# Another engine for some tiles of the first batch, and an uneven split of the last output tile

## The chip, the cores and the metric

One core of a Trainium2 chip. The metric is device time in microseconds (us), lower is better. The kernel before takes 251.05 us (median of three runs, 250.95 to 251.22).

## The reference, cut to what matters

```python
a = softmax(phi)                                   # 8 batches, 8 heads, 576 rows, 32 memory slots
k_m, v_m = a^T k, a^T v                            # per head 32 x 64
x = softmax(q k_m^T / 8) v_m                       # -> [8, 576, 512]
out = x + relu(layernorm(x) @ w_ch1) @ w_ch2       # 512 -> 2048 -> 512
```

The kernel never forms layernorm(x) @ w_ch1 directly: it folds v_m and w_ch1 into one small matrix per batch (w1b) and multiplies that by the attention weights (Eh). The result, the 2048-wide hidden layer, is made in 16 tiles of 128 hidden units by 576 rows.

## The kernel before

The hidden tiles, and who empties them:

```python
def mm1(b, j0, j1):
    for j in range(j0, j1):
        h_ps = big([P, 2, 512], FP32, "h_ps")      # PSUM, 3 buffers in all for this tag
        ... 4 matmuls of 128 x 288 from w1b and Eh ...                        # L405
        if j % 3 or j == 0:
            nc.scalar.activation(out=dst, in_=h_ps[:, :, 0:HS], func=AF.Relu) # L411, ScalarE
        else:
            nc.vector.tensor_scalar(out=dst, in0=h_ps[:, :, 0:HS], ... max 0) # L413, VectorE
```

The first batch has no work before it to hide behind. It alternates parts of the folding with hidden tiles; the folding products use the same three buffers, and VectorE empties them (L388):

```python
mm1(0, 0, 2)
w1_mean(2); m_copy(2); a_w1b(0, 1)    # mean of w1 by TensorE, copied by ScalarE; folding: TensorE, then VectorE
mm1(0, 2, 5)
w1_mean(3); m_copy(3); a_w1b(0, 2)
mm1(0, 5, 8)
w1_mean(4); m_copy(4); a_w1b(0, 3)
a_vb(0)                               # L281, two short VectorE passes, wanted by x_tiles
mm1(0, 8, 16)
x_tiles(0, [0, 1]); x_tiles(0, [2, 3])
mm2(0, 0, 0, 4) ...                   # L474, "the long product": 40 matmuls, output tiles 0, 1 and half of 2
a_kv(1); a_tr(1); a_qT(1, 0) ...      # batch 1's k and v, then its q in two halves, as their loads land
```

The loads go in one order through GpSimd's queue: q, k, v of batch 0, w1 in five pieces, w2 in four, then phi, k, v and the two halves of q of batch 1, then batch 2. A finished output tile is stored from SyncE's queue (mm2_out). The last tile is made in two halves of 256 columns (mm2_last), so that the first half is stored while the second is computed.

The softmax here doesn't subtract the row's maximum and nothing guards it: scores larger than these inputs give would overflow.

## Time and profile before

| | before |
|---|---|
| time, median of 3 | 251.05 us |
| span of the profiled execution | 248.5 us |
| the profiled execution's own time | 250.3 us |
| TensorE busy | 96% |
| share of TensorE in the chain that ended last | 88% |

The chain is the work that ended last, followed back to what released each step. The lines themselves stand in the prediction.

### The profile page before, as it was taken

Reading aid. Unit: us, or ns where it says so; the run is one execution under the profiler, and the core shown is the slowest. Engines: PE = TensorE matmul, PEld = TensorE weight load, DVE = VectorE, ACT = ScalarE, POOL = GpSimd, SP = SyncE. Lnnn points to the kernel's source line nnn. Section 1 sums busy time; section 2 is a strip of 40 time slices with the busy share of each in tenths; the row PEclk is TensorE's granted clock in tenths of the full one; section 3 lists DMA queues with packets and bytes.
Section 4 is the critical chain, followed back from the end, with each engine's and each line's share of the span. In section 5 each row is a group of like instructions: output and inputs, shape, how many; then the busy total and the mean of one; then the engine's idle time right before and its main releaser. Section 6 shows DMA issues by size and latency. Waiting matters only on the chain.

```text
span 248.5 us, 5893 instructions
## 1 busy us (share of the span) xinstructions
PE 238.5 (96%) x2491; PEld 132.5 (53%) x2491; DVE 156.2 (63%) x304; ACT 130.0 (52%) x219; POOL 60.6 (24%) x100
## 2 busy tenths in 40 slices
PE   7879999999999999999999999999999999999993
PEld 2444555557544665467544774467444764476453
DVE  3246663785578646686569547785679538783641
ACT  3165572587463555736472646655680755465210
POOL 8643241032515402090206202170205011000000
PEclk9999999999999999999999999999999999999999
DMA  7999999998599899829975995539983302103133
GB/s 151 195 202 207 206 257 208 291 222 148 119 200 210 122 218 242 160 38 201 251 127 112 158 245 136 122 38 223 209 158 77 80 7 46 42 17 70 42 84 84
DMA packets 42450, 36.82 MB, mean 148 GB/s; under 512 B 17460, under 2 KB 37688, under 8 KB 42424
## 3 DMA queue, kind: packets, MB, share of 16 engines
q0 software_dynamic: 17776, 19.53, 46.9%
q1 hardware_dynamic: 24488, 16.79, 29.3%
q8 instruction: 19, 0.31, 0.5%
q10 hardware_dynamic: 160, 0.13, 0.2%
q14 instruction: 7, 0.06, 0.1%
HBM read 41.42 MB, written 9.44 MB: 205 GB/s over the span
## 4 chain that ended last, share of the span: by engine, by line
PE 88%; DMA 4%; DVE 2%; ACT 2%; POOL 1%; issue 1%; DVEq 0%; POOLq 0%
PE ch_ps L474 50%; PE h_ps L405 25%; DMA kv_bf<-in_v_dram 4%; PE w1b_ps L384 3%; PE kv_ps L210 2%; PE o_ps L435 2%; PE last_ps L486 1%; PE sc_ps L322 1%; PE m_ps L165 1%; ACT rT L411 1%; PE den_ps L353 1%; DVE w1b L388 1%; POOL q_bf L92 1%; ACT E_sb L327 1%; POOL kv_bf L84 1%
## 5 line engine op out<-in xcount | busy, mean ns | idle before, releaser
L474 PE MATMUL ch_ps<-w2b,rT 128*128 128x512 bf16 x560 | 128.4, 380 | 0.0
L474 PEld LDWEIGHTS <-rT 128*128 128x128 bf16 x560 | 52.0, 98 | 63.5 <-issue 6.5
L405 PE MATMUL h_ps<-Eh,w1b 128*128 128x288 bf16 x512 | 66.6, 286 | 1.3 <-ACT rT L411 1.2
L411 ACT ACTIVATE rT<-h_ps 128x576 bf16<-128x576 f32 x88 | 52.4, 648 | 28.7 <-PE h_ps L405 28.7
L405 PEld LDWEIGHTS <-w1b 128*128 128x128 bf16 x512 | 49.5, 97 | 18.3 <-issue 2.6
L388 DVE SCALAR_TENSOR_TENSOR w1b<-m_sb,rsum,w1b_ps 128x512 bf16<-128x512 f32 (+1 forms) x66 | 44.2, 726 | 9.6 <-PE w1b_ps L384 5.3
L413 DVE TENSOR_SCALAR rT<-h_ps 128x576 bf16<-128x576 f32 x40 | 30.3, 757 | 24.9 <-PE h_ps L405 24.3
L498 DVE SCALAR_TENSOR_TENSOR x_sb<-ch_ps,rstd,x_sb 128x512 f32<-128x512 f32 x35 | 26.1, 746 | 9.9 <-PE ch_ps L474 9.1
L454 DVE BATCH_NORM_STATS2 bst<-x_sb 128x6 f32<-128x512 f32 x36 | 24.4, 678 | 7.6 <-ACT x_sb L441 7.6
L441 ACT ACTIVATE x_sb<-o_ps 128x1024 f32<-128x1024 f32 (+1 forms) x20 | 17.5, 938 | 18.4 <-PE o_ps L435 18.4
L281 POOL TENSOR_TENSOR vb<-v,vmask 128x256 bf16<-128x256 bf16 x12 | 7.7, 663 | 60.1 <-DVE rs L237 60.1
L194 POOL TENSOR_TENSOR es<-e_sb 128x512 f32<-128x512 bf16 x6 | 6.9, 1156 | 62.9 <-ACT e_sb L187 62.9
L460 ACT ACTIVATE rstd<-mv,eps_sb 128x2 f32<-128x2 f32 (+1 forms) x20 | 5.9, 297 | 30.4 <-DVE mv L455 30.2
L327 ACT ACTIVATE E_sb<-sc_ps,rs 128x640 bf16<-128x640 f32 x16 | 11.8, 790 | 12.4 <-PE sc_ps L322 12.4
L369 DVE SCALAR_TENSOR_TENSOR Eh<-E_sb,rs,rden 128x576 bf16<-128x576 bf16 x16 | 12.4, 815 | 8.8 <-ACT rden L368 8.8
L384 PE MATMUL w1b_ps<-w1r,kvT 64*32 64x512 bf16 (+1 forms) x264 | 10.9, 374 | 0.0
L179 PE MATMUL w_ps<-fill 128*128 128x512 f32 (+1 forms) x16 | 9.4, 699 | 1.6 <-DVE fill L119 1.6
L227 DVE CAST k<-kv_ps 128x256 bf16<-128x256 f32 x7 | 3.0, 425 | 12.5 <-PE kv_ps L210 12.5
L187 ACT ACTIVATE e_sb<-phi_st 128x1152 bf16<-128x1152 f32 x8 | 9.2, 1151 | 2.6 <-DMA phi_st<-in_phi_dram 2.6
L368 ACT ACTIVATE rden<-rden 128x576 f32<-128x576 f32 x16 | 10.0, 672 | 0.1
L92 POOL DMA_DIRECT2D q_bf<-in_q_dram x10 | 7.6, 756 | 4.6 <-DMA w2b<-in_moe_w_ch_dram 1.8
L210 PE MATMUL kv_ps<-kv_bf,e_sb 64*32 64x128 bf16 (+1 forms) x648 | 7.4, 215 | 0.6 <-DMA kv_bf<-in_v_dram 0.3
(76 smaller groups left out, 151.3 us busy)
## 6 DMA issues: line engine op xcount, KB each, us to landing
out_dram<-x_sb SPq DMA_DIRECT2D x70, 128.0 KB, 2.8
kv_bf<-in_k_dram POOLq DMA_DIRECT2D x7, 576.0 KB, 6.1
kv_bf<-in_v_dram POOLq DMA_DIRECT2D x7, 576.0 KB, 9.2
phi_st<-in_phi_dram SPq DMA_DIRECT2D x6, 576.0 KB, 6.1
q_bf<-in_q_dram POOLq DMA_DIRECT2D x6, 576.0 KB, 13.9
w2b<-in_moe_w_ch_dram POOLq DMA_DIRECT2D x4, 512.0 KB, 17.7
w1r<-in_moe_w_ch_dram POOLq DMA_DIRECT2D x3, 512.0 KB, 13.8
q_bf<-in_q_dram POOLq DMA_DIRECT2D x4, 288.0 KB, 12.4
```

The source lines that it names most:

```text
L210: nc.tensor.matmul(ps[32 * j:32 * (j + 1), g, 0:D * (sl.stop - sl.start)], e[r:r + TS, c, j, :], kv[r:r + TS, j, sl, D * c:D * (c + 1)], s ...
L327: nc.scalar.activation(out=E_[:, g].rearrange("p (a x) -> p a x", a=2), in_=sc[:, :, 0:HP], func=AF.Exp, scale=s["rs"][:, g:g + 1])
L369: nc.vector.scalar_tensor_tensor(out=Eh[:, g, :], in0=s["E"][:, g, 0:S], scalar=s["rs"][:, g:g + 1], in1=rd[:, g].rearrange("p a x -> p (a ...
L384: nc.tensor.matmul(ps[32 * j:32 * (j + 1), g, 0:N], s["kvT"][r:r + 64, 2, 32 * j:32 * (j + 1)], w1r[r:r + 64, j, fs], start=True, stop=Tru ...
L388: nc.vector.scalar_tensor_tensor(out=s["w1b"][:, g, fs], in0=m_sb[:, fs], scalar=s["rsum"][:, g:g + 1], in1=ps[:, g, 0:N], op0=ALU.mult, o ...
L405: nc.tensor.matmul(h_ps[:, half, 0:HS], s["w1b"][:, g, P * j:P * (j + 1)], s["Eh"][:, g, HS * half:HS * (half + 1)], start=(g == 0), stop= ...
L411: nc.scalar.activation(out=dst, in_=h_ps[:, :, 0:HS], func=AF.Relu)
L413: nc.vector.tensor_scalar(out=dst, in0=h_ps[:, :, 0:HS], scalar1=0.0, scalar2=None, op0=ALU.max)
L441: nc.scalar.activation(out=x[:, 0:n].rearrange("p i (u y) -> p i u y", u=2), in_=o_ps.rearrange("p u (i y) -> p i u y", i=2)[:, 0:n], func ...
L454: nc.vector.bn_stats(out=stt, in_=x)
L474: nc.tensor.matmul(ch_ps, rT[:, j, P * t:P * (t + 1)], w2b[:, j, :], start=(j == 0), stop=(j == JC - 1))
L498: nc.vector.scalar_tensor_tensor(out=x, in0=ch_ps, scalar=rstd, in1=x, op0=ALU.mult, op1=ALU.add)
```

## The change

Its intent: VectorE folds twice between groups of hidden tiles, and the tiles that it also empties come right behind its folding, so that they wait. It is to take tiles 1, 4, 7, 10, 13 instead of 3, 6, 9, 12, 15 (batch 0 alone), and the two short passes for vb move behind tile 10. At the end, a part of 384 columns and then one of 128 leave less to do after the last matmul.

```diff
-            if j % 3 or j == 0:
+            if j % 3 != 1 if b == 0 else j % 3 or j == 0:
                 nc.scalar.activation(out=dst, ...)
...
-        for n in range(2):
+        for cs in (slice(0, 384), slice(384, 512)):
             ps = big([P, 2, 512], FP32, "last_ps")
-            cs = slice(256 * n, 256 * (n + 1))
+            N = cs.stop - cs.start
...  (256 becomes N in the matmul and in VectorE's pass)
     a_w1b(0, 3)
+    mm1(0, 8, 11)
     a_vb(0)
-    mm1(0, 8, 16)
+    mm1(0, 11, 16)
```

More of the change, by code (lines that the diff above doesn't have):

```diff
@@ L481, in mm2_last @@
         x, rstd = xs[(pr, t)]
-        for n in range(2):
+        for cs in (slice(0, 384), slice(384, 512)):
             ps = big([P, 2, 512], FP32, "last_ps")
-            cs = slice(256 * n, 256 * (n + 1))
+            N = cs.stop - cs.start
             for j in range(JC):
-                nc.tensor.matmul(ps[:, 0, 0:256], pair[pr][:, j, P * t:P * (t + 1)], w2b[:, j, cs],
+                nc.tensor.matmul(ps[:, 0, 0:N], pair[pr][:, j, P * t:P * (t + 1)], w2b[:, j, cs],
                                  start=(j == 0), stop=(j == JC - 1))
-            nc.vector.scalar_tensor_tensor(out=x[:, cs], in0=ps[:, 0, 0:256], scalar=rstd,
+            nc.vector.scalar_tensor_tensor(out=x[:, cs], in0=ps[:, 0, 0:N], scalar=rstd,
                                            in1=x[:, cs], op0=ALU.mult, op1=ALU.add)
```

## The prediction

> **What bounds the kernel now.** I read the page first: the share of busy time, then the chain of work that ended last.
>
> ```profile
> PE 238.5 (96%) x2491; PEld 132.5 (53%) x2491; DVE 156.2 (63%) x304; ACT 130.0 (52%) x219; POOL 60.6 (24%) x100
> ...
> PE 88%; DMA 4%; DVE 2%; ACT 2%; POOL 1%; issue 1%; DVEq 0%; POOLq 0%
> ```
>
> TensorE carries 88% of the chain; the second line says so, the first only that it is busy. So a change gains only where TensorE waits, or before its first and after its last matmul. Page, chain and waits put the waits in the first batch and the end. The list of waits for TensorE has one that this change is about:
>
> ```profile
> PE h_ps L405 <- ACT rT L411: 1.2, 5, 0.2
> ```
>
> Then the timeline of the first batch (start, length, engine, line, operation, count, idle before), from tile 8 of its 16 hidden tiles on:
>
> ```profile
> 28.98 1.41 DVE L388 SCALAR_TENSOR_TENSOR w1b<-m_sb,rsum,w1b_ps 128x512 bf16<-128x512 f32 x2 [1.11 <-ACT m_sb L174]
> 29.29 0.65 ACT L411 ACTIVATE rT<-h_ps 128x576 bf16<-128x576 f32 x1 [0.34 <-PE h_ps L405]
> 29.99 1.14 PE L405 MATMUL h_ps<-Eh,w1b 128*128 128x288 bf16 x8 [0.25 <-ACT rT L411]
> ...
> 30.31 0.49 DVE L281 TENSOR_TENSOR vb<-v,vmask 128x256 bf16<-128x256 bf16 x2
> 30.68 1.19 ACT L411 ACTIVATE rT<-h_ps 128x576 bf16<-128x576 f32 x2 [0.74 <-PE h_ps L405]
> 30.71 0.75 DVE L413 TENSOR_SCALAR rT<-h_ps 128x576 bf16<-128x576 f32 x1
> ...
> 31.38 2.15 PE L405 MATMUL h_ps<-Eh,w1b 128*128 128x288 bf16 x16 [0.25 <-ACT rT L411]
> ```
>
> A tile is four matmuls into one of three PSUM buffers; ScalarE or VectorE empties it, and only then may a later tile use that buffer. The instruction record gives 0.121 us from one matmul's start to the next, so 0.485 us a tile, and the first reader's start 0.69 us after the tile's. A reader keeps the buffer 0.65 us (ScalarE) or 0.75 us (VectorE); TensorE goes on 0.05 us later. "0.25 idle" is counted from modelled ends; in starts, the matmul at 31.38 follows the one at 30.84, where 30.96 was possible: 0.42 us lost. The same stands at 23.39 (0.41, and 0.21 more for its second half at 23.85, which waits for the folded weights), 26.80 (0.41) and 29.99 (0.41): 1.86 us in four places.
>
> The end, from the timeline of the last 10 us:
>
> ```profile
> 241.05 3.66 PE L486 MATMUL last_ps<-w2b,rT 128*128 128x256 bf16 x32
> 244.74 0.48 DVE L488 SCALAR_TENSOR_TENSOR x_sb<-last_ps,rstd,x_sb 128x256 f32<-128x256 f32 x1 [1.21 <-PE last_ps L486]
> ```
>
> After the last matmul, VectorE's 0.48 us and one store (issued at 245.25, landed at 247.2 on one queue and 247.45 on the other) are bare time.
>
> [...]0.25 us idle in each of four places, each ended by the reader of a buffer. [...]its ten 128-column transposes at 44.85, each with a weight load, stand 55.5 ns apart. [...]the last two stores, 64 KB each, took 1.95 and 2.19 us.
>
> **Part 1: who empties the first batch's tiles.** VectorE had tiles 3, 6, 9, 12, 15 and gets 1, 4, 7, 10, 13; five each, so nothing is added or removed. I went through the built order of both programs, which shows which reader each tile waits for, and put the durations above to it.
>
> Tiles 0 to 3 run as before: tile 1's reader ends at 21.65 in place of 21.60, and nobody waits for it. Tile 4 waits for tile 2's reader, tile 7 for tile 5's, tile 10 for tile 8's. Tiles 2, 5 and 8 are ScalarE's before and after, and start when they did (22.69, 26.10, 29.29): ScalarE's copies of the mean, at 21.76, 25.17 and 28.35, still wait for the matmuls in front of them. So three of the four stalls stay: 0.41 + 0.21 + 0.41 + 0.41 = 1.44 us.
>
> The fourth goes. Before, tile 9 (VectorE) waits behind the fold and behind vb, from 29.74 to 30.71, so tile 12 takes the buffer of tile 10 and waits for its reader to 31.33. Changed, ScalarE reads tile 9 at 29.84 to 30.49, VectorE reads tile 10 at 30.68 to 31.43, and tile 12 waits for tile 9, long done: it starts at 30.96, 0.42 us earlier. Behind it: tile 13 waits for tile 10 (31.48, where 31.45 was possible); tile 14 at 31.97 waits for tile 11's reader (31.17 to 31.82); tile 15 at 32.46 for tile 12's (31.72 to 32.37): free. vb moves behind tile 10 and ends near 31.83, before tile 13 is ready at 32.13. The products after it take tile 13's buffer (VectorE 32.17 to 32.92) and then tile 14's (ScalarE to 33.31): the second half starts near 33.36 in place of 33.80. So the next matrix product starts at about 33.69, not 34.13: 0.44 us earlier.
>
> **Part 2: what of it survives.** The same TensorE work follows, until batch 1's products with k and v at 43.07. They'd start at 42.63, but v's load lands at 42.74, on a queue that is full throughout (the page's DMA row is at 9 there) and waits for nothing that this change moves. So TensorE waits to about 42.79 and 0.28 us is left. The first half of batch 1's q lands at 44.53, its use moves from 44.85 to 44.57: just in time (its second half, landed 46.33, is wanted at 46.53). The stores that share the engines start 0.44 us earlier and may hold these loads up a little, so I count 0.25. Later loads have over a microsecond, and the chain from 53.5 to 241 is TensorE with the same waits, so this is carried to the end.
>
> **Part 3: the last tile in 384 and 128 columns.** TensorE before: 32 x 0.1095 = 3.50 us. After: 16 x 0.1625 (between 256 and 512 columns) + 16 x 0.0555 = 3.49: even. The last matmul's own length falls from 0.273 to 0.220 us (the transposes'), but it starts 0.05 later. VectorE's last pass: 484 - 128 x 1.04 = 351 ns, 0.13 us less. The store: four packets of 1 KB on each DMA engine and queue, 75 ns each; at 512 bytes half of that saves some 0.15 of about 2 us; as two queues share the engines I count 0.08. The 384 part's issue ends near 245.0, before the second's at 245.11. Together 0.21 us.
>
> **Sum.** 0.25 + 0.21 = 0.46 us; 251.05 - 0.46 = 250.6 us, 0.2%.
>
> **Rivals.** (a) *All stalls go, as the change intends*: 1.86 + 0.21, some 249.0 us. For it: the four stalls are all put down to ScalarE. Against it: the three readers that end three of them don't change. Even then the loads for batch 1 would hold TensorE at 42.74, so it could not last. (b) *The loads take it all*: if the earlier stores push v and q back by 0.2 us or more, part 1 gives 0 to 0.1 and the time is 250.8 to 251.0. For it: queues full from 20 to 54 us. Against it: the stores issued at 39.5 move no data until 43.0 by the DMA records, after v. (c) *vb or VectorE becomes the wait*: if VectorE is 0.4 us late with tile 13, the products behind it wait and part 1 is gone: 250.85. Against it: 0.3 us of slack by the working above. [...](e) *No DMA limit*: all of 0.44 stays, 250.4.
>
> **Range and chances.** (b), (d) and (e) span 250.4 to 251.0; three runs of before spread by 0.27 us. I take 250.15 to 251.05. Two per cent is 5 us, over twice what even (a) gives, and no part can cost that: within 2% at 0.98, the rest shared.
>
> **What would show it.** In the changed profile: idle before the first batch's tiles still three times, at 23.4, 26.8 and 30.0, with ScalarE named, and none near 31.4; the long product starts at 33.7; a wait of TensorE for v of batch 1 near 42.7, new in the list of waits; from there everything about 0.25 us earlier; last_ps x32 as long as before; VectorE's last pass near 0.35 us; the last store a little under 2 us. I'm wrong if the stalls at 26.8 or 30.0 are gone, if v lands earlier too, or if the 128-column matmuls stand over 60 ns apart.

What the prediction took from outside this case is cut out of it, and with it rival (d), that a 128-column matmul would take longer in the last tile than in the transposes. No term of the sum is cut: it came to 0.25 + 0.21 = 0.46 us, and the range stands without (d) too, since (b) as it was written reaches 251.0. What part 3 reckons with is in the trace of before: starts of matmuls 0.109 us apart at 256 columns (L486) and 0.216 at 512 (L474); VectorE's pass from PSUM 750 ns at 512 columns (L498) and 484 at 256 (L488), so 1.04 ns a column, and 218 ns if that line is drawn on to none; a store's packets of 2 KB 154 ns on SyncE's queue, those of 1 KB 75 there and 68 on ScalarE's (medians). The 0.03 us taken off for the stores in part 2, and the 0.15 and 0.08 us for the smaller store in part 3, are estimates.

## The result, and the profile after

| | before | changed |
|---|---|---|
| median | 251.0 us (4 runs, 250.94 to 251.22) | 250.12 us (4 runs, 249.78 to 250.62) |
| profiled execution | 250.3 us, span 248.5 | 249.78 us, span 248.0 |

The ratio is 0.9965 (95% interval 0.9947 to 0.9983). Ratios in this text are the mean time of one kernel's fast runs over that of the other's of the same rounds, so not quite the ratio of the medians. 250.12 lies 0.03 us under the predicted range. The medians are 0.88 us apart, the two profiled executions 0.52.

The shares of busy time and of the chain, after:

```profile
PE 239.1 (96%) x2491; PEld 132.3 (53%) x2491; DVE 156.5 (63%) x304; ACT 129.7 (52%) x219; POOL 60.6 (24%) x100
...
PE 79%; DMA 17%; DVE 1%; issue 1%; POOL 1%; ACT 1%; POOLq 0%
```

Busy time is as before, the chain is not: DMA has gone from 4% to 17%. The steps of the chain from 10 us to TensorE's first, in order of time (start, length, what), show where that is:

```profile
10.13 14.78 DMA w1r<-in_moe_w_ch_dram
24.91 0.29 issue
25.20 19.28 DMA q_bf<-in_q_dram
44.48 0.05 issue
44.52 0.73 PE qT_ps L304 x10
```

Before, the chain ran over TensorE with short steps of the other engines from 13 us on. Now it runs over the loads up to batch 1's q, which lands at 44.48, and TensorE takes it up 0.04 us later. The list of TensorE's waits (total, times, longest) has that wait as a new line, and the stall of the first batch went from 1.2 to 1.0 us:

```profile
PE h_ps L405 <- ACT rT L411: 1.0, 4, 0.2
...
PE qT_ps L304 <- DMA q_bf<-in_q_dram: 0.2, 1, 0.2
```

The timeline of the first batch from tile 8 on, as in the prediction:

```profile
29.07 1.19 ACT L411 ACTIVATE rT<-h_ps 128x576 bf16<-128x576 f32 x2 [0.34 <-PE h_ps L405]
29.77 3.13 PE L405 MATMUL h_ps<-Eh,w1b 128*128 128x288 bf16 x24 [0.25 <-ACT rT L411]
30.46 0.76 DVE L413 TENSOR_SCALAR rT<-h_ps 128x576 bf16<-128x576 f32 x1 [0.29 <-PE h_ps L405]
...
31.14 0.48 DVE L281 TENSOR_TENSOR vb<-v,vmask 128x256 bf16<-128x256 bf16 x2
...
33.48 8.81 PE L474 MATMUL ch_ps<-w2b,rT 128*128 128x512 bf16 x40
```

The stall before tile 10 (0.25 idle, at 29.77 now) is still there, and behind it 24 matmuls run without a break where there were 8, a stall, and 16. And the end:

```profile
240.65 3.66 PE L486 MATMUL last_ps<-w2b,rT 128*128 128x384 bf16 x32
...
244.35 0.35 DVE L488 SCALAR_TENSOR_TENSOR x_sb<-last_ps,rstd,x_sb 128x128 f32<-128x128 f32 x1 [0.22 <-PE last_ps L486]
```

TensorE's 32 matmuls take 3.66 us in both kernels, VectorE's last pass 0.35 in place of 0.48.

For comparing runs I cut each trace at six places, all read from the instruction records and the record of DMA completions. Below, "head" is the first batch's part of the change (readers and vb), "end" that of the last tile, K to Q the stretch in which batch 1's q is wanted. The places: v0, the landing of the second half of batch 0's v; M, the third matmul of tile 0; L, the start of the long product; K, batch 1's first product with k and v; Q, the first transpose of the second half of batch 1's q; E, the first matmul of the last tile.

| us | v0 lands | M | M to L | L to K | K to Q | Q to E | E to end |
|---|---|---|---|---|---|---|---|
| before | 14.51 | 19.96 | 14.17 | 8.94 | 3.73 | 194.24 | 7.45 |
| changed | 14.03 | 19.74 | 13.74 | 8.94 | 3.98 | 194.25 | 7.33 |

The head gains 0.43 (M to L), gives back 0.25 at q (K to Q), and the end gains 0.12; the other 0.22 us is M itself. Batch 0's loads had landed earlier by 0.48 us, and 0.22 of that was left at M. No instruction before M differs between the two kernels. So part of even these 0.52 us is not the change's. One of the prediction's own signs of being wrong also came up, "v lands earlier too": it landed at 42.31, not 42.74, but counted from v0 it came 28.28 us later, before 28.23. The wait for v that was to be new isn't in this trace; the one for q is.

### The profile page after: what moved, and what is told of

It is laid out like the page before. It is cut to its first block, busy times and chain, and to the rows that moved or that the text cites. A ratio compares the mean times of both kernels' runs of the same rounds, so it can differ in the third digit from the quotient of the medians.

```text
span 248.0 us, 5893 instructions
## 1 busy us (share of the span) xinstructions
PE 239.1 (96%) x2491; PEld 132.3 (53%) x2491; DVE 156.5 (63%) x304; ACT 129.7 (52%) x219; POOL 60.6 (24%) x100
## 4 chain that ended last, share of the span: by engine, by line
PE 79%; DMA 17%; DVE 1%; issue 1%; POOL 1%; ACT 1%; POOLq 0%
PE ch_ps L474 46%; PE h_ps L405 22%; DMA q_bf<-in_q_dram 8%; DMA w1r<-in_moe_w_ch_dram 6%; DMA kv_bf<-in_k_dram 3%; PE w1b_ps L384 3%; PE kv_ps L210 2%; PE last_ps L486 1%; PE o_ps L435 1%; PE sc_ps L322 1%; PE den_ps L353 1%; POOL q_bf L92 1%; DVE k L227 1%; PE qT_ps L304 0%; ACT qT L307 0%
## 5 line engine op out<-in xcount | busy, mean ns | idle before, releaser
L474 PE MATMUL ch_ps<-w2b,rT 128*128 128x512 bf16 x560 | 128.4, 380 | 0.0
L474 PEld LDWEIGHTS <-rT 128*128 128x128 bf16 x560 | 52.1, 98 | 63.4 <-issue 6.4
L498 DVE SCALAR_TENSOR_TENSOR x_sb<-ch_ps,rstd,x_sb 128x512 f32<-128x512 f32 x35 | 26.1, 746 | 9.6 <-PE ch_ps L474 8.8
L179 PE MATMUL w_ps<-fill 128*128 128x512 f32 (+1 forms) x16 | 10.3, 759 | 1.6 <-DVE fill L119 1.6
L358 ACT ACTIVATE rden<-den_ps 64x576 f32<-64x576 f32 x12 | 7.7, 644 | 0.2
```

Of the source, the lines that this page charges most:

```text
L179: nc.tensor.matmul(w_ps[:, 0:N], fill[:, 0:P], fill[:, 0:N], start=True, stop=True)
L474: nc.tensor.matmul(ch_ps, rT[:, j, P * t:P * (t + 1)], w2b[:, j, :], start=(j == 0), stop=(j == JC - 1))
L498: nc.vector.scalar_tensor_tensor(out=x, in0=ch_ps, scalar=rstd, in1=x, op0=ALU.mult, op1=ALU.add)
```

## The experiments

Theory: the sizes of the parts are about as predicted, batch 1's loads take most of what the head gains, and single runs differ by the start of their loads. The first rival: a term is mis-sized and 0.9 us is real. Each has six runs unless told otherwise, and the experiments of one set of rounds share eleven runs of the kernel before. There are eighteen experiments; the sets ran on different chips.

### One part at a time: e1 to e4

e1 is the changed kernel again. e2 has the new head alone, e3 the new end alone, and e4 only the new readers, with vb where it was:

```diff
 # e2: mm2_last as before        # e3: reader test and a_vb as before
 # e4: mm2_last as before and
-    mm1(0, 8, 11)
     a_vb(0)
-    mm1(0, 11, 16)
+    mm1(0, 8, 16)
```

> The changed kernel once more, unaltered. Theory A (the sizes I predicted are right, 0.46 us, and the 0.9 us of the first measurement is the spread of single runs, whose start-up loads landed up to 0.5 us apart in the two profiles): 0.3 to 0.6 us under the kernel before. Theory B (a term is mis-sized, 0.9 us is real): 0.8 to 1.0 us under it.

> The first batch's readers and the place of vb as changed, the last tile in two halves of 256 as before. Theory A: 0.25 us under the kernel before, and the long product after the first batch starts 14.17 - 0.44 = 13.73 us after tile 0's third matmul. Theory B1 (the head is mis-sized: the whole stall survives, or more): 0.5 to 0.7 us under it.

> The last tile in 384 and 128 columns alone, the first batch as before. Theory A: 0.2 us under the kernel before, 0.13 of it in VectorE's last pass (0.48 to 0.35 us). Theory B2 (the tail is mis-sized, the smaller store saves more): 0.4 us or more under it.

> Only which engine empties which tile of the first batch; vb stays in front of tiles 8 to 15. By the dependencies vb ends at 30.7 where tile 10 is ready at 30.64, so VectorE takes tile 10 at 30.72 in place of 30.68: Theory A says as e2 within 0.05 us, the move of vb is worth nothing. The rival that vb in VectorE's way is what cost the stall says: the stall near 31.4 is still there and the gain of e2 is gone.

| | median, us | range | ratio to before, 95% |
|---|---|---|---|
| before (11 runs) | 250.42 | 250.21 to 251.87 | |
| e1 changed | 250.47 | 249.38 to 251.63 | 0.9989 (0.9960 to 1.0017) |
| e2 head alone | 251.19 | 250.30 to 251.65 | 1.0010 (0.9986 to 1.0034) |
| e3 end alone | 250.46 | 249.97 to 251.03 | 0.9990 (0.9968 to 1.0012) |
| e4 readers alone | 250.42 | 250.18 to 251.17 | 0.9996 (0.9971 to 1.0020) |

The 0.88 us did not come back, and the times decide nothing: runs of one kernel lie up to 2.25 us apart. The traces do decide:

| us | v0 lands | M to L | v lands | L to K | K to Q | Q to E | E to end |
|---|---|---|---|---|---|---|---|
| e1 | 14.78 | 13.74 | 43.34 | 9.42 | 4.21 | 194.22 | 7.29 |
| e2 | 14.74 | 13.74 | 42.87 | 8.97 | 3.93 | 194.23 | 7.45 |
| e3 | 14.74 | 14.17 | 43.37 | 9.07 | 4.16 | 194.22 | 7.31 |
| e4 | 14.16 | 13.77 | 42.71 | 9.37 | 4.21 | 194.23 | 7.45 |

M to L is 13.74 to 13.77 with the new readers and 14.17 without: the head gives 0.40 to 0.43 us, and the place of vb is worth 0.03 of it (e4). E to end is 7.29 to 7.33 with the new end and 7.45 without. Q to E is the same in all, within 0.03 us. All that is left to differ is between L and Q, where TensorE waits for loads, and where everything starts. TensorE's timeline of e1 around K shows the wait, with what ended it:

```profile
42.61 0.37 PE L218 MATMUL kv_ps<-ones,e_sb 128*128 128x2 bf16 x9
43.38 0.80 PE L210 MATMUL kv_ps<-kv_bf,e_sb 64*32 64x128 bf16 x72 [0.41 <-DMA kv_bf<-in_v_dram]
...
45.10 0.22 PE L264 MATMUL kvT_ps<-ident,v 128*128 128x128 bf16 x1
45.46 0.73 PE L304 MATMUL qT_ps<-ident,q_bf 128*128 128x128 bf16 x10
```

The product with v begins at 43.38, 0.04 us after v landed. In this run v alone took back all that the head had gained (L to K is 0.48 longer than 8.94), and q took more. e3 has the old head and waits as well, 0.13 for v and 0.43 for q: the kernel before is at this limit too, in some runs, though not in its own trace.

### The loads made smaller and larger: e5, e6, e8, e9, e10

If loads take the head's gain, it must come back when they land early. e5 (old head and end) and e6 (changed kernel) don't load k of batch 1, and use v in its place. Their outputs are wrong, which doesn't matter for the times. e9 and e10 are the same two once more. e8 is the changed kernel with 256 KB more to load, for nothing.

```diff
 # e5, e6, e9, e10
-        for slot, src in ((0, k), (1, v)):
+        for slot, src in ((0, k), (1, v))[b == 1:]:
...
-                        kv[r:r + TS, j, sl, D * c:D * (c + 1)],
+                        kv[r:r + TS, j, 1:2, D * c:D * (c + 1)].to_broadcast([TS, 2, D]) if b == 1 else ...
 # e8, in front of batch 1's phi
+    junk = consts.tile([P, 2, C], BF16, name="junk")
+    nc.gpsimd.dma_start(out=junk, in_=w2_v[:, 0:2, :])
```

> The kernel before, with batch 1's k not loaded (its products with k use v instead: a wrong result on purpose), so that v and q of batch 1 land 2.6 us earlier. Theory L (up to batch 1's q the kernel's pace is set by its loads, whose start differs by up to 0.9 us from run to run): no wait for v or q is left, so tile 0's third matmul to batch 1's first product with v takes 23.11 us as in the trace of before, and the time falls by 0 to 0.7 us, as much as the single run of before waited for loads. Rival N (the head's gain is lost to something else than loads, or was never there): the time stays as it is.

> The changed kernel with batch 1's k not loaded, as e5. Theory L: now the head keeps all of its 0.44 us: tile 0's third matmul to batch 1's first product with v takes 22.67 us, and the interval to the last tile's first matmul is 0.44 us shorter than in e5; with the end's 0.14 us the span from that matmul is 0.58 us under e5's. Rival N: no shorter than e5's, or by 0.1 to 0.2 only.

> The changed kernel with 256 KB of w2 loaded once more, for nothing, in front of batch 1's phi (about 1.27 us at the queue's 0.2 MB per us). Theory L: everything from batch 1's q on moves by that, and the span is the landing of q's second half + 201.55 us as in the profile of e1, so some 1.1 to 1.3 us slower than the changed kernel. Rival N (loads are hidden): within 0.3 us of it.

> e5 again, as the profile of e5 fell in a run in which the first weights landed 1.7 us late and the granted clock dropped to 0.50 from 18 to 23 us. Theory L (loads of batch 1 swallow the head's gain): no wait for v or q; tile 0's third matmul to the long product 14.17 us, from there to the product with v 8.94, to q's second half 3.73, 194.23 from there to the last tile. Mean time over the rounds 0.5 to 0.6 us above e10's. Rival N: the two don't differ by more than the end's 0.14.

> e6 again, for the times. Theory L: intervals 13.74, 8.94, 3.73 and 194.23 us and the end 7.31, as in e6; over the rounds 0.5 to 0.6 us under e9. Rival N: within 0.14 of it.

The rate in e8's expectation is that of before: 207 GB/s in the windows from 18 to 23 and from 38 to 43 us. The 2.6 us in e5's is an estimate; counted from v0, v came 2.5 us earlier in e9 than in before, and 2.8 to 2.9 earlier in e6 and e10 than in the changed kernel.

| us | v0 lands | M | M to L | v lands | L to K | K to Q | Q to E | E to end | median |
|---|---|---|---|---|---|---|---|---|---|
| e9, old | 14.44 | 19.83 | 14.17 | 40.16 | 8.94 | 3.73 | 194.24 | 7.45 | 250.36 |
| e6, changed | 14.31 | 19.77 | 13.74 | 39.68 | 8.94 | 3.73 | 194.24 | 7.31 | 250.11 (4 runs) |
| e10, changed | 14.52 | 19.98 | 13.74 | 39.96 | 8.94 | 3.74 | 194.24 | 7.30 | 250.51 |
| e8, changed + load | 14.96 | 20.42 | 13.74 | 45.52 | 11.40 | 3.74 | 194.94 | 7.32 | 253.02 (2 runs) |

With v in early, L to K and K to Q are at their least in both heads, and M to E is 0.43 us shorter in the changed kernel (e6 and e10 against e9): the head's whole gain. TensorE's waits of e6 name no wait for v or q of batch 1. In e8 the load goes straight into the time: the product with v waits 2.46 us, by the list of waits

```profile
PE kv_ps L210 <- DMA kv_bf<-in_v_dram: 0.6, 1, 0.6
```

for e6, where that one is batch 0's, and for e8

```profile
PE kv_ps L212 <- DMA kv_bf<-in_v_dram: 3.1, 2, 2.4
```

e8 became slower than I expected (253.02; its v landed 30.56 us after v0, against 27.8 to 28.7 in the other traces that load k, and 0.7 us more was lost later, 0.6 of it in a wait for a transposed q). The stores of tiles 0 and 1 began to move data at 43.40, 2.1 us before its v was in, which may be why v came that late; this was not tested. But its direction is the theory's, and far outside the rival's 0.3 us. The times of e9 and e10, 250.36 and 250.51, do not show the 0.57 us that their traces do: three of e10's six runs, and one of e9's, had a mean granted clock of 0.992 or 0.993, and the runs with 0.996 and more are 249.71, 249.73 and 250.32 in e10 against 250.14 to 250.89 in e9. With e5's and e6's runs added by the same cut it is 250.39 for the old head and end (8 runs) and 250.05 for the changed kernel (7). That choice of runs was made after seeing them, so it is a hint and no proof.

e5 (253.65, 250.66, 250.58 and 249.91 us) has no row above, since the clock dropped in its trace; e16 below shows the same. Both profiled runs took over 252.9 us at a mean clock of 0.986. That the runs at 0.992 are of this kind too was not traced. TensorE's timeline of e16 and the windows from 18 to 23 us of e16 and of before (columns: length, busy time of TensorE, its weight loads, VectorE, ScalarE, GpSimd, granted clock, DMA share, GB/s):

```profile
17.55 1.01 PE L165 MATMUL m_ps<-w1r,gneg 128*128 128x256 bf16 x4 [0.88 <-DMA w1r<-in_moe_w_ch_dram]
```

```profile
18.00:23.00 5.00, 5.00 (x31) 2.61 (x30) 3.55 (x7) 0.83 (x2) 2.02 (x3) 0.50 1.24 207
```

```profile
18.00:23.00 5.00, 4.74 (x42) 2.77 (x42) 3.30 (x7) 2.81 (x6) 1.50 (x2) 1.00 1.24 207
```

The first piece of w1 landed at 17.51 us, 2.88 after v0; in the eighteen traces without a drop that is 1.32 to 1.34. TensorE idled 0.88 us, from 16.67 on, and its clock was granted at half from 16.92 to 23.75 us. In e5 TensorE waited 0.9 us for the same piece, and the mean granted clock was 0.89 from 14 to 18 us and 0.50 from 18 to 23. Such a drop, with TensorE at work, came in these two of twenty traces (mean clock 0.986; 0.997 to 1.0 in the others); what sets it off is not shown. In e16 M comes 8.04 us after v0 in place of 5.46: 1.55 of these 2.6 us is the weights' own delay. The instructions up to M are those of the kernel before.

### Room for the loads: e7, e11, e12, e17, e18

Batch 1's q lands while the stores of output tiles 0 and 1 move data. e7 is the changed kernel with these stores sent behind batch 2's loads, in GpSimd's queue. e11 is e7 with two of output tile 2's matmuls in front of batch 1's products, and e12 is e11 with the old head. e17 and e18 (the same kernel) keep the stores in SyncE's queue and put them behind that of tile 2. The results are right.

```diff
 # e7, e11, e12, e17, e18: mm2_out(0, 0) and mm2_out(0, 1) without their stores
     load(2)
+    x_store(0, 0, nc.gpsimd)      # e7, e11, e12
+    x_store(0, 1, nc.gpsimd)
 # e11, e12
-    mm2(0, 2, 0, 8)
+    mm2(0, 2, 0, 10)
     a_kv(1)
-    mm2(0, 2, 8, 12)
+    mm2(0, 2, 10, 12)
 # e17, e18
     mm2_out(0, 2)
+    x_store(0, 0, nc.sync)
+    x_store(0, 1, nc.sync)
```

> The changed kernel with the stores of output tiles 0 and 1 sent through GpSimd's queue behind batch 2's loads, so that they take no DMA time from batch 1's q; same result. Theory L: the halves of q land 1.3 to 1.4 us apart in place of 1.8 to 2.1, the second 0.5 to 0.8 us earlier after v than in the changed kernel (4.0 us after v there), and the time falls 0.2 to 0.4 us under the changed kernel's. Rival: the stores don't hold q up, or v's landing alone sets the pace: no change.

> e7 with two of the third tile's matmuls (0.43 us) moved in front of batch 1's products with k and v; same result. Theory L: TensorE works there where it waited for v, v's wait falls from 0.4 to under 0.1 us, q is in time, nothing else moves, and the time from the landing of batch 0's v (second half) to the last tile falls from 226.5 (e7) to some 226.2 us, 0.6 under the changed kernel's mean of 226.8. Rival: the chain of steps behind v is the bound from there on, the two matmuls are missing later as filling, and nothing is gained over e7.

> e11 with the first batch as in the kernel before (VectorE takes tiles 3, 6, 9, 12, 15). Theory L: with room in front of v neither head waits for loads by much, so this is 0.3 to 0.44 us slower than e11 from the landing of batch 0's v to the last tile: 226.5 to 226.6 us. Rival: as fast as e11, since the loads still take the head's gain.

> The changed kernel with the stores of output tiles 0 and 1 left on SyncE's queue but behind tile 2's, which comes at 49.7 us, so that no store takes DMA time from batch 1's q; same result. Theory L: no wait for q (from the product with v to q's second half 3.73 us in place of 3.74 to 4.21), the end 7.30 and not 7.55 as with GpSimd's queue (e7), from the landing of batch 0's v to the last tile 226.1 to 226.6 us, and a mean 0.1 to 0.2 us under the changed kernel's. Rival: the stores come due later and are in the way of batch 2's loads or of the buffers, and the intervals after q grow by as much.

> The same kernel as e17 once more, since one set of six runs has an uncertainty of 0.2 us in its mean: the same intervals (3.73 us from the product with v to q's second half, 7.30 at the end), and the mean of both sets 0.4 to 0.6 us under the kernel before.

| us | v to q's halves landing | L to K | K to Q | v0 to E | E to end | median | ratio, 95% |
|---|---|---|---|---|---|---|---|
| e7 | 1.41 and 1.42 | 9.36 | 3.73 | 226.53 | 7.55 | 250.32 | 0.9980 (0.9950 to 1.0011) |
| e11 | 1.41 and 1.40 | 9.37 | 3.65 | 226.43 | 7.57 | 250.60 | 0.9991 (0.9972 to 1.0011) |
| e12, old head | 1.41 and 1.42 | 9.37 | 3.64 | 226.87 | 7.58 | 251.07 | 1.0005 (0.9989 to 1.0022) |
| e17 | 1.48 and 1.45 | 8.94 | 3.73 | 226.09 | 7.33 | 250.27 | 0.9999 (0.9972 to 1.0026) |
| e18 | 1.41 and 1.42 | 8.94 | 3.74 | 226.10 | 7.30 | 250.35 | 0.9979 (0.9963 to 0.9994) |

Without those stores the halves of q land 1.40 to 1.48 us apart; with them 1.63 to 2.28 in before, changed, e1 to e4 and e13 to e15, and the wait at q is gone: K to Q is 3.73 or 3.74 in e7, e17 and e18, in e7 although v was late. Where the stores stay but move no data until q is in (e6, e9, e10, e16), the halves land 1.41 to 1.49 us apart as well. So the stores make that wait. TensorE's timeline of e17, with no idle time before either of the two (v landed at 42.78, q's first half at 44.26):

```profile
42.89 0.80 PE L210 MATMUL kv_ps<-kv_bf,e_sb 64*32 64x128 bf16 x72
...
44.67 0.72 PE L304 MATMUL qT_ps<-ident,q_bf 128*128 128x128 bf16 x10
```

v's landing is not theirs: e7 still waited 0.42 us for v, in e17 and e18 v happened to be in time. e11's filling costs what it gives: K comes 0.43 us later whether v is late or not (v had landed 0.69 us before it), and only 0.08 returns. e12 against e11 shows the head again, 226.87 to 226.43. The 0.25 us that GpSimd's queue adds at the end is SyncE's: it tests the queues' semaphores one after the other, some 0.06 us each by the instruction records (at 246.95, 247.01 and 247.08 us in the changed kernel), and in e7 seven of these stood behind the last landing, in the changed kernel three.

e11 (226.2 expected) and e12 (226.5 to 226.6) missed their intervals, and e7's time did not fall under the changed kernel's. e17 and e18 together have twelve runs with a mean of 250.50 us, 0.33 under the kernel before of their rounds (0.4 to 0.6 was expected), the changed kernel 250.53 over 21. Their traces have the shortest way from v0 to E of the kernels with a right result, but one changed run (e14) was as short; by time they are not shown to be better.

### How much of the head is kept in the ordinary run: e13 to e16

The end alone (e13, e15) and the whole change (e14, e16), unaltered copies of e3 and e1.

> The end alone, as e3, for its times and one more trace of the old head under ordinary loads. From the landing of batch 0's v to the last tile 226.5 us (no wait for loads) to 227.1 (v and q late), as the two traces of the old head so far. Theory L: the mean of these is at most 0.2 above that of the changed kernel's. Theory H (the head keeps most of its 0.43 us in the ordinary run too): 0.35 or more above.

> The changed kernel, as e1. Theory L: 226.3 to 227.1 us from the landing of batch 0's v to the last tile, with waits for v or q; the mean time within 0.2 us of e13's. Theory H: 226.1 to 226.3 and 0.35 us or more faster than e13.

> As e13, once more: 226.5 to 227.1 us from the landing of batch 0's v to the last tile; by theory L within 0.2 us of the changed kernel, by theory H 0.35 us or more above it.

> As e14, once more: by theory L 226.3 to 227.1 us from the landing of batch 0's v to the last tile, with waits for v or q, and within 0.2 us of e15; by theory H 226.1 to 226.3.

| us | v0 lands | M to L | v lands | L to K | K to Q | v0 to E | E to end | median |
|---|---|---|---|---|---|---|---|---|
| e13, end alone | 14.31 | 14.17 | 42.81 | 8.94 | 3.87 | 226.68 | 7.34 | 250.40 (5 runs) |
| e14, changed | 14.65 | 13.74 | 42.44 | 8.94 | 3.74 | 226.11 | 7.30 | 250.40 (5 runs) |
| e15, end alone | 14.92 | 14.17 | 43.15 | 8.94 | 3.73 | 226.52 | 7.30 | 250.52 |
| e16, changed | 14.63 | 14.27 (clock) | 43.24 | 8.94 | 3.73 | 229.21 | 7.30 | 250.66 |

Theory L's intervals held in e13 and e15, e14 fell in theory H's, and in e16 the clock dropped; by mean times the changed kernel was 0.19 us faster (e14) and 0.29 slower (e16) than the end alone beside it. So these four alone don't decide. e14's v landed 27.79 us after v0, early enough for nothing to wait, and there the whole 0.43 is kept; e1 and e4 kept nothing. Old head, four traces without a clock drop (before, e3, e13, e15): v0 to E 226.52 to 227.05, mean 226.70. New head, five (changed, e1, e2, e4, e14): 226.11 to 227.03, mean 226.63. So the ordinary run keeps 0.07 of 0.43 us by the traces, with a standard error of 0.22: nothing is not excluded, nor, at two errors, all of it. The times narrow it: over all timed runs the mean is 250.89 for before (59 runs), 250.59 for the end alone (17), 250.53 for the changed kernel (21), with standard errors of 0.07, 0.11 and 0.16, and 250.82 for the head alone (e2 and e4, 12 runs, 0.14). The head is then worth 0.05 beside the new end and 0.07 beside the old one, each with a standard error of 0.15 to 0.2, together some 0.06 with 0.12. All of 0.43 is three errors away, as far as runs on different chips may be put together. The whole change is worth about 0.35 us, give or take 0.35 (twice the combined error).

## Why the prediction was wrong

**The step that failed is the last one**, the range, and with it the sum, which has no term for where the work starts: "three runs of before spread by 0.27 us. I take 250.15 to 251.05". Over all its 59 runs the kernel before spreads from 250.21 to 252.44, and the changed one from 249.38 to 252.92. A median of four such runs moves by some tenths of a microsecond, and the first one fell low, by luck: the same kernel's later medians are 250.47, 250.40 and 250.66, all inside the range. Part of the spread is the start. The page's DMA row is at 9 from 6 us to batch 1's q, the first batch can't start before its loads have landed (M is 5.4 to 5.5 us behind v0 in all traces without a clock drop but the first of the changed kernel, where it is 5.71), and v0 landed anywhere from 14.03 to 14.96 us. Another part goes with the granted clock: of the 55 runs of the kernel before in the experiments' rounds, ten have a mean of 0.990 to 0.992 and average 251.67 us; the other 45, at 0.997 and more, average 250.70 (250.21 to 251.37). The profiled execution at 250.3 us could have warned me. I took a spread from three runs that were close by chance.

**The head, 0.44 us earlier: right.** Three stalls stay and the fourth goes, as worked out from who reads tiles 2, 5, 8 and 9; measured 0.43. The long product was predicted at 33.69, and starts at 33.48, with M 0.22 earlier.

**What survives of it, 0.25: the mechanism right, the size taken from one landing.** "v's load lands at 42.74, on a queue that ... waits for nothing that this change moves": the traces agree (from v0 to v 28.40 us on the mean of the four old heads, 28.26 for the five new), but one trace's landing was used as if it were fixed. Counted from v0, v lands 27.8 to 28.7 us later (e8 with its extra load left out), the new head wants it 28.14 us after v0 (5.46 + 13.74 + 8.94) and the old one at 28.57. That interval lies inside the spread, so a run keeps anything from nothing to all of the gain; the mean measured 0.07 in the traces. The stores' part, counted as 0.03, measured 0 to 0.48 us at q (K to Q 3.73 to 4.21), old head and new.

**The end, 0.21: over-sized by the store.** TensorE even (3.66 both) and VectorE's pass 0.13 shorter (350 ns at 128 columns; the 617 at 384 lies on the line of 484 and 750 as well): right, and 16 matmuls of 128 columns run 56 ns apart. The store's 0.08 didn't come: from the end of VectorE's pass to the end of the span it is 3.27 us before and 3.28 after. The transfer on ScalarE's queue took 2.13 us in place of 2.19, but ScalarE began it 0.11 us after the pass, not 0.03, with its first store only just issued: the 384 part's issue ended at 244.71, and VectorE's last pass at 244.70, where the prediction had room between them. On SyncE's queue the smaller store took longer, 2.05 us in place of 1.94. The end measured 0.12 to 0.16.

**The rivals.** (a), all stalls go, fell by the three that are left. (b), the loads take it all, is what happened in e1 and e4; (e), all is kept, in e14; both are true of single runs. (c) fell: the head gave 0.43 of the 0.44 us, with vb in its old place 0.40 (e4). So did (d): the 128-column matmuls stood 56 ns apart, as the transposes do. One sum in (b) is off: with 0 to 0.1 for part 1 and 0.21 for the end the time is 250.74 to 250.84, not 250.8 to 251.0.

In sum: predicted 0.46 us from parts of 0.25 and 0.21; measured 0.07 and some 0.14 in the traces, and 0.35 in the times with an uncertainty as large. What part of the 0.88 us of the first measurement was a matter of these four and four runs can't be told more closely than that.

## What to carry to other kernels

Before a stall on the busiest engine is counted as time, ask what the next thing is that this engine waits for if it comes there earlier: here a queue of loads stood 0.3 us behind, and on average took most of what the stall gave back. Where loads are that close, a time read from one trace is one draw of many; cut several traces at the same instructions, and compare the intervals between these rather than the totals. And take a range from the spread of what sets the pace, not from three runs that agree.
